# RMS norm of 16384 rows on one core: the whole of x kept in SBUF, the gain multiplied first, the row scale written back over x, and every mean square but the first two rows' on ScalarE

## The chip, the cores and the metric

One core of one Trainium2 chip runs the program. The metric is the device time of one execution in microseconds (us); several runs are given by their median. Names of engines in the rows: PE is TensorE, DVE is VectorE, ACT is ScalarE, POOL is GpSimd, SP is SyncE, which only issues transfers here.

## What is computed

The reference, cut to what matters. x is 512x32x640 and g is 640, both bfloat16:

```python
rms = jnp.sqrt((x * x).mean(axis=-1, keepdims=True) + 1e-6)
return x / rms * g
```

So each of the 16384 rows of 640 numbers is divided by the root of its mean square, and multiplied by g column by column. x is 20.97 MB, read once, and the output is as large, written once.

## The kernel before

The 16384 rows are laid out 128 to a step: partition p holds rows 128p to 128p+127 of x, and what is called a **row** below is one such step, 128 partitions x 640 bfloat16 (1280 bytes a partition, 163.84 KB in all). There are 128 of them. `chunk_schedule` cuts them into 19 chunks of 2, 4, 4, fourteen times 8, 4 and 2 rows. For each chunk the loop at L154 does this:

- **Load** (L92, L159, issued by SP): a chunk goes into one of 6 buffers `x_sb_full`. From the seventh load on SP waits until the buffer's earlier chunk has been read by DVE and PE.
- **Mean squares**, one row at a time, into a column of `ms`. Most rows go by PE and ACT: two matmuls with an identity matrix (L200 and L203, 512 and 128 columns) copy the row into one of 3 PSUM tiles `xp`, and ACT squares that with an accumulated sum (L209), its elementwise result going to a throw-away SBUF tile `junk_a`. 24 of the 128 rows (`n_dve`, L162 to L172) go to DVE instead, as one `scalar_tensor_tensor` (L187).
- **1/rms**: ACT takes the root (L231, into `rstd`), DVE the reciprocal (L233).
- **Scale**: DVE multiplies each row by its 1/rms (L143, one `tensor_scalar` a row, into `o_sb_full`, 3 buffers) and then the whole chunk by g in place (L145, one `tensor_tensor` a chunk).
- **Store**: one transfer a chunk, issued by POOL (L149), by SP for the last three chunks (L147).

g is loaded as one row and spread over the partitions by a matmul with ones (L119) and two copies on ACT (L122). The order on each engine is not written out: the tile framework's scheduler chooses it, and so a `scalar_tensor_tensor` of one chunk may stand between the steps of another. ACT, DVE and PE run their instructions strictly in that order.

Of the kernel before, what the change touches and what calls it, by code (L numbers as in the profile page):

```python
# [6 lines left out]

# [3 lines left out]
J_MAX = int(os.environ.get("K_J", "8"))
RAMP = [int(v) for v in os.environ.get("K_RAMP", "2,4").split(",") if v]
DRAMP = [int(v) for v in os.environ.get("K_DRAMP", "4,2").split(",") if v]
DVE_SS_EVERY = float(os.environ.get("K_DVE_EVERY", "6"))
FRONT = [int(v) for v in os.environ.get("K_FRONT", "2,2,2").split(",") if v]
NODVE_LAST = int(os.environ.get("K_NODVE_LAST", "3"))
IO_BUFS = int(os.environ.get("K_BUFS", "6"))
O_BUFS = int(os.environ.get("K_OBUFS", "3"))
S_BUFS = int(os.environ.get("K_SBUFS", "4"))  # L20
OUT_ENG = os.environ.get("K_OUTENG", "gpsimd")
IN_ENG = os.environ.get("K_INENG", "sync")
G_ENG = os.environ.get("K_GENG", "sync")
LASTOUT_SYNC = int(os.environ.get("K_LASTOUT_SYNC", "3"))
GBC = os.environ.get("K_GBC", "pe_act")
X0FIRST = int(os.environ.get("K_X0FIRST", "2"))
PAIR = int(os.environ.get("K_PAIR", "0"))
WARM_SQRT = int(os.environ.get("K_WARM", "1"))
XPSUM = int(os.environ.get("K_XPSUM", "3"))


def chunk_schedule(R):
    start = list(RAMP)
    end = list(DRAMP)
    if sum(start) + sum(end) > R:
        start, end = [], []
    rem = R - sum(start) - sum(end)
    mid = []
    while rem >= J_MAX:
        mid.append(J_MAX)  # L40
        rem -= J_MAX
    if rem:
        mid = [rem] + mid
    sizes = start + mid + end
    assert sum(sizes) == R
    return sizes
# [3 lines left out]
def kernel(  # L50
# [16 lines left out]
    assert N % P == 0, f"{N=} must be a multiple of {P}"  # L67
# [5 lines left out]
    sizes = chunk_schedule(R)
    JM = max(sizes)
    nchunks = len(sizes)
# [4 lines left out]
    junk_pool = ctx.enter_context(tc.tile_pool(name="junk", bufs=int(os.environ.get("K_JBUFS", "8"))))  # L80
    small = ctx.enter_context(tc.tile_pool(name="small", bufs=S_BUFS))

    engines = {"sync": nc.sync, "scalar": nc.scalar, "gpsimd": nc.gpsimd, "vector": nc.vector}
    in_eng = engines[IN_ENG]
    out_eng = engines[OUT_ENG]

    pre_x = {}
    r0p = 0
    for ci0 in range(min(X0FIRST, nchunks)):
        J0 = sizes[ci0]  # L90
        x_sb_full0 = xin_pool.tile([P, JM, D], xf.dtype, name="x_sb_full")
        in_eng.dma_start(out=x_sb_full0[:, :J0, :], in_=x_v[:, r0p:r0p + J0, :])  # L92
        pre_x[ci0] = x_sb_full0
        r0p += J0

    eps_sb = consts.tile([P, 1], f32)
    nc.vector.memset(eps_sb[:], EPS)  # L97

    if WARM_SQRT:
        warm = consts.tile([P, 1], f32)  # L100
        nc.vector.memset(warm[:], 1.0)
        warm2 = consts.tile([P, 1], f32)
        nc.scalar.activation(out=warm2[:], in_=warm[:], func=ACT.Sqrt, bias=eps_sb[:], scale=1.0)  # L103

    g_sb = consts.tile([P, D], g.dtype)
    if GBC == "dma":
        g_src = bass.AP(tensor=g.tensor, offset=g.offset, ap=[[0, P], g.ap[-1]])
        engines[G_ENG].dma_start(out=g_sb[:], in_=g_src)
    else:
        g1 = consts.tile([1, D], g.dtype)  # L110
        g_row = bass.AP(tensor=g.tensor, offset=g.offset, ap=[[0, 1], g.ap[-1]])
        engines[G_ENG].dma_start(out=g1[:], in_=g_row)  # L112
        ones1 = consts.tile([1, P], bf16)
        nc.vector.memset(ones1[:], 1.0)
        gps_pool = ctx.enter_context(tc.tile_pool(name="gps", bufs=1, space=bass.MemoryType.PSUM))
        half = D // 2
        for h in range(2):
            gp = gps_pool.tile([P, half], f32, name=f"gp{h}")
            nc.tensor.matmul(out=gp[:], lhsT=ones1[:], rhs=g1[:, h * half:(h + 1) * half],  # L119
                             start=True, stop=True)  # L120
            if GBC == "pe_act":
                nc.scalar.copy(out=g_sb[:, h * half:(h + 1) * half], in_=gp[:])  # L122
            else:
                nc.vector.tensor_copy(out=g_sb[:, h * half:(h + 1) * half], in_=gp[:])

    if XPSUM:
        from concourse.masks import make_identity
        ident = consts.tile([P, P], bf16, name="ident")
        make_identity(nc, ident)
        xps_pool = ctx.enter_context(tc.tile_pool(name="xps", bufs=XPSUM, space=bass.MemoryType.PSUM))  # L130

# [137 lines left out]
```

## Time and profile before

| what | value |
|---|---|
| time, median of 6 runs | 119.71 us (119.22 to 120.71) |
| the profiled execution: time | 119.74 us |
| the profiled execution: span from first to last instruction | 118.0 us |
| DVE busy | 102.9 us, 87% of the span, 217 instructions |
| ACT busy | 78.6 us, 67%, 231 instructions |
| PE busy | 59.8 us, 51% |
| POOL busy | 11.2 us, 9% |
| DMA | 42.00 MB, 356 GB/s over the span |
| read and written in HBM | 20.97 MB each |
| mean granted TensorE clock | 0.703 of full speed |

A view of the profile either sums over the span (busy time of each engine, groups of instructions by line), or cuts it into stretches, or lists instructions in order of time with the idle time before each and what ended it. The busy time of an instruction includes its start-up and its end, in which the next one already runs: what an engine needs for a series is the distance from start to start, not the sum of the busy times.

### The profile page before, as it was taken

What the parts mean: (1) busy time and instruction counts of PE and PEld (TensorE: products, weight loads), DVE (VectorE), ACT (ScalarE), POOL (GpSimd) and SP (SyncE); (2) the same over time, 40 slices, a digit from 0 to 9 for tenths busy, and PEclk for the clock granted to TensorE, in tenths of its full rate; (3) what the DMA queues carried; (4) which work ended last, traced back from release to release, by engine and by line L of the source; (5) the groups of instructions that cost most, each with busy time, mean ns of one, the idle gap of its engine ahead of it and who ended that gap; (6) DMA issues with size and microseconds to landing.
All of it is one profiled execution on the core that took longest, in us unless ns stands there. A gap on an engine that the chain in (4) does not pass through costs nothing.

```text
span 118.0 us, 1065 instructions
## 1 busy us (share of the span) xinstructions
PE 59.8 (51%) x210; PEld 23.2 (20%) x210; DVE 102.9 (87%) x217; ACT 78.6 (67%) x231; POOL 11.2 (9%) x22
## 2 busy tenths in 40 slices
PE   0244889655895593969492859484993000000000
PEld 0011333222332221323131323132331000000000
DVE  0598998999999999998949957959699999999870
ACT  5076699999999995979695979697999120000000
POOL 2002021010101010100101010010020102033000
PEclk9999999999769955555559555569559655555555
DMA  3999999999999999999999999999719190825994
GB/s 90 344 347 410 394 425 424 422 430 432 431 417 434 434 422 413 441 437 406 434 441 433 406 441 434 417 422 443 249 56 396 58 389 0 358 87 222 431 373 196
DMA packets 5415, 42.00 MB, mean 356 GB/s; under 512 B 609, under 2 KB 610, under 8 KB 1826
## 3 DMA queue, kind: packets, MB, share of 16 engines
q1 hardware_dynamic: 3170, 23.27, 48.5%
q0 software_dynamic: 2240, 18.68, 37.7%
...
HBM read 20.97 MB, written 20.97 MB: 356 GB/s over the span
## 4 chain that ended last, share of the span: by engine, by line
issue 52%; DVE 14%; DMA 12%; ACT 12%; POOL 4%; SPq 1%; PE 1%; POOLq 0%
ACT junk_a L209 11%; DMA x_sb_full<-in_x_dram 8%; DVE o_sb_full L145 7%; DVE o_sb_full L143 5%; POOL out_dram L149 4%; DMA out_dram<-o_sb_full 4%; DVE junk_d L187 1%; SPq L92 1%; PE xp L200 1%; ACT rstd L231 0%; DVE rstd L233 0%; SPq L159 0%; SPq L112 0%; POOLq L149 0%; PE xp L203 0%
## 5 line engine op out<-in xcount | busy, mean ns | idle before, releaser
L209 ACT ACTIVATE junk_a<-xp 128x640 bf16<-128x640 f32 x104 | 72.1, 764 | 9.9 <-PE xp L203 9.8
L200 PE MATMUL xp<-x_sb_full,ident 128*128 128x512 bf16 x104 | 52.7, 528 | 24.8 <-DMA x_sb_full<-in_x_dram 16.2
L145 DVE TENSOR_TENSOR o_sb_full<-o_sb_full,g_sb 128x5120 bf16<-128x5120 bf16 (+2 forms) x19 | 45.4, 2391 | 0.0
L143 DVE TENSOR_SCALAR o_sb_full<-x_sb_full,rstd 128x640 bf16<-128x640 bf16 x128 | 39.8, 380 | 0.4 <-DVE o_sb_full L143 0.4
L203 PE MATMUL xp<-x_sb_full,ident 128*128 128x128 bf16 x104 | 29.3, 282 | 0.0
L209 ACT ACTIVATION_READ_ACCUMULATOR junk_a<-xp 128x1 f32 x104 | 28.0, 269 | 0.0
L187 DVE SCALAR_TENSOR_TENSOR junk_d<-x_sb_full 128x640 bf16<-128x640 bf16 x24 | 19.1, 801 | 3.2 <-DMA x_sb_full<-in_x_dram 3.1
L200 PEld LDWEIGHTS <-ident 128*128 128x128 bf16 x104 | 13.4, 129 | 41.1 <-DMA x_sb_full<-in_x_dram 19.5
L149 POOL DMA_DIRECT2D out_dram<-o_sb_full x16 | 10.5, 655 | 95.3 <-DVE o_sb_full L145 66.8
L203 PEld LDWEIGHTS <-ident 128*128 128x128 bf16 x104 | 11.4, 110 | 20.1 <-issue 19.8
L231 ACT ACTIVATE rstd<-ms,eps_sb 128x8 f32<-128x8 f32 (+2 forms) x19 | 5.9, 327 | 8.3 <-DVE junk_d L187 8.3
L233 DVE RECIPROCAL rstd<-rstd 128x8 f32<-128x8 f32 (+2 forms) x19 | 3.4, 187 | 7.1 <-ACT rstd L231 7.1
L119 PE MATMUL gp_88<-g_81,ones_83 1*128 1x320 bf16 x1 | 0.4, 419 | 5.2 <-DMA g_81<-in_g_dram 5.2
L187 DVE DVE_READ_ACCUMULATOR junk_d<-x_sb_full 128x1 f32 x24 | 2.0, 81 | 0.0
L103 ACT ACT_TABLE_LOAD x1 | 1.3, 1283 | 0.7 <-PEq L253 0.7
L119 PEld LDWEIGHTS <-ones_83 1*128 1x128 bf16 x2 | 0.2, 99 | 5.1 <-issue 4.0
L97 DVE MEMSET eps_sb<- 128x1 f32 x1 | 0.1, 59 | 0.8 <-PEq L253 0.8
L119 PE MATMUL gp_91<-g_81,ones_83 1*128 1x320 bf16 x1 | 0.5, 466 | 0.0
L122 ACT CAST g_sb<-gp_91 128x320 bf16<-128x320 f32 x1 | 0.4, 427 | 0.0
L122 ACT CAST g_sb<-gp_88 128x320 bf16<-128x320 f32 x1 | 0.4, 405 | 0.0
L103 ACT ACTIVATE warm_78<-warm,eps_sb 128x1 f32<-128x1 f32 x1 | 0.3, 295 | 0.0
masks.py:199 POOL TENSOR_SCALAR_AFFINE_SELECT ident<-ident 128x128 bf16<-128x128 bf16 x1 | 0.3, 287 | 0.1
(7 smaller groups left out, 0.8 us busy)
## 6 DMA issues: line engine op xcount, KB each, us to landing
...
```

What stands on the lines that cost most here:

```text
L92: in_eng.dma_start(out=x_sb_full0[:, :J0, :], in_=x_v[:, r0p:r0p + J0, :])
L103: nc.scalar.activation(out=warm2[:], in_=warm[:], func=ACT.Sqrt, bias=eps_sb[:], scale=1.0)
L119: nc.tensor.matmul(out=gp[:], lhsT=ones1[:], rhs=g1[:, h * half:(h + 1) * half], start=True, stop=True)
L143: nc.vector.tensor_scalar_mul(out=o_sb[:, j, :], in0=x_sb[:, j, :], scalar1=rstd[:, roff + j:roff + j + 1])
L145: nc.vector.tensor_tensor(out=o_sb, in0=o_sb, in1=g_bcast(J), op=ALU.mult)
L149: out_eng.dma_start(out=o_v[:, r0:r0 + J, :], in_=o_sb)
L187: nc.vector.scalar_tensor_tensor(out=junk_d[:], in0=x_sb[:, j, :], scalar=inv_d, in1=x_sb[:, j, :], op0=ALU.mult, op1=ALU.mult, accum_out= ...
L200: nc.tensor.matmul(out=xp[:, :c1], lhsT=ident[:], rhs=x_sb[:, j, :c1], start=True, stop=True)
L203: nc.tensor.matmul(out=xp[:, c1:], lhsT=ident[:], rhs=x_sb[:, j, c1:], start=True, stop=True)
L209: nc.scalar.activation(out=junk_a[:], in_=sq_in, func=ACT.Square, scale=inv_sqrt_d, accum_out=ms[:, moff + j:moff + j + 1],)
L231: nc.scalar.activation(out=rstd[:, :J], in_=ms[:, :J], func=ACT.Sqrt, bias=eps_sb[:], scale=1.0)
L233: nc.vector.reciprocal(out=rstd[:, :J], in_=rstd[:, :J])
```

## The change

The kernel is rewritten. What each part does:

- **Loads**: 13 tiles `x0` to `x12`, one for each load, hold all 128 rows for the whole run. The loads are of 2, 4, 4, 8, six times 16, 8, 4 and 2 rows; a load of 16 rows is two chunks, so the chunks are the same 19 as before. No load waits for a buffer.
- **Mean squares**: the two rows of chunk 0 stay on DVE (L102). The other 126 go through PE and ACT. ACT's square writes its elementwise result over `xp` in PSUM, in float32, in place of an SBUF tile, and its sum into a PSUM tile `ms`. The root (L123) reads `ms` from PSUM.
- **Scale**: DVE multiplies a chunk by g first, from x into a buffer `y` (L129, 3 buffers), which needs no mean square; then it multiplies each row of `y` by 1/rms (L136) into the place that the row of x had.
- **Store**: from the x tiles, all 19 by POOL (L137).
- **Order**: written by hand for PE, DVE, SP and POOL. DVE does `times_g` of chunk c, and then `finish` of chunk c-1.

```diff
+LOADS = [
+    [2], [4], [4], [8], [8, 8],
+    [8, 8], [8, 8], [8, 8], [8, 8],
+    [8, 8], [8], [4], [2],
+]
...
-    xin_pool = ctx.enter_context(tc.tile_pool(name="xin", bufs=IO_BUFS))
-    out_pool = ctx.enter_context(tc.tile_pool(name="xout", bufs=O_BUFS))
...
+    xin = ctx.enter_context(tc.tile_pool(name="xin", bufs=1))
+    ypool = ctx.enter_context(tc.tile_pool(name="ypool", bufs=3))
...
+    xps = ctx.enter_context(tc.tile_pool(name="xps", bufs=3, space=bass.MemoryType.PSUM))
+    mps = ctx.enter_context(tc.tile_pool(name="mps", bufs=2, space=bass.MemoryType.PSUM))
...
+    ctx.enter_context(tc.manual_schedule(
+        engines={ENG.PE, ENG.DVE, ENG.SP, ENG.Pool}))
...
+    for i, cuts in enumerate(LOADS):
+        n = sum(cuts)
+        t = xin.tile([P, n, D], xf.dtype, name=f"x{i}")
+        nc.sync.dma_start(out=t[:], in_=x_v[:, r0:r0 + n, :])
+        if i == 0:
+            nc.sync.dma_start(out=g1[:], in_=g_row)
...
+    def sumsq(c):
+        xs, J, _ = chunks[c]
+        if c == 0:
...
+        ms = mps.tile([P, JM], f32, name="ms")
...
         for j in range(J):
+            xp = xps.tile([P, D], f32, name="xp")
+            for lo, hi in ((0, 512), (512, D)):
+                nc.tensor.matmul(out=xp[:, lo:hi], lhsT=ident[:], rhs=xs[:, j, lo:hi],
+                                 start=True, stop=True)
+            sq = nc.scalar.activation(out=xp[:], in_=xp[:], func=ACT.Square, scale=inv_sqrt_d,
+                                      accum_out=ms[:, j:j + 1])
...
+    def times_g(c):
+        xs, J, _ = chunks[c]
+        y = ypool.tile([P, JM, D], bf16, name="y")
+        nc.vector.tensor_tensor(out=y[:, :J, :], in0=xs, in1=g_bcast(J), op=ALU.mult)
+        return y
 
+    def finish(c, y, r):
+        xs, J, r0 = chunks[c]
+        nc.vector.reciprocal(out=r[:, :J], in_=r[:, :J])
+        for j in range(J):
+            nc.vector.tensor_scalar_mul(out=xs[:, j, :], in0=y[:, j, :], scalar1=r[:, j:j + 1])
+        nc.gpsimd.dma_start(out=o_v[:, r0:r0 + J, :], in_=xs)
...
+    prev = None
+    for c in range(len(chunks)):
+        ms = sumsq(c)
+        y = times_g(c)
+        r = rms(c, ms)
+        if prev is not None:
+            finish(*prev)
+        prev = (c, y, r)
+    finish(*prev)
```

Three places of the order of instructions follow. First DVE in the middle of the program, before, over two chunks of 8 rows:

```order
L233 RECIPROCAL rstd<-rstd 128x8
L187 SCALAR_TENSOR_TENSOR junk_d,ms<-x_sb_full 128x640
L143 TENSOR_SCALAR o_sb_full<-x_sb_full,rstd 128x640 x8
L187 SCALAR_TENSOR_TENSOR junk_d,ms<-x_sb_full 128x640
L145 TENSOR_TENSOR o_sb_full<-o_sb_full,g_sb 128x5120
L233 RECIPROCAL rstd<-rstd 128x8
```

And DVE in the changed program at the same place (the numbers tell the tiles apart: `x4_93` is the tile of the fifth load, `x5_95` that of the sixth):

```order
L129 TENSOR_TENSOR y_306<-x4_93,g_sb_117 128x5120
L134 RECIPROCAL rstd_261<-rstd_261 128x8
L136 TENSOR_SCALAR x4_93<-y_259,rstd_261 128x640 x8
L129 TENSOR_TENSOR y_353<-x5_95,g_sb_117 128x5120
L134 RECIPROCAL rstd_308<-rstd_308 128x8
L136 TENSOR_SCALAR x4_93<-y_306,rstd_308 128x640 x8
```

The two `scalar_tensor_tensor` between the steps of a chunk are gone, and the product with g has moved ahead of the root: `y_353`, a chunk of the next load, stands before the reciprocal and the eight row scales of the chunk ahead of it.

Second, SP's loads from the fifth on, before, with the semaphores that each waits for (DMAHW and DMASW are those of transfers that SP and POOL issued):

```order
L159 DMA x_sb_full<-in_x_dram 128x5120 x3
L159 DMA x_sb_full<-in_x_dram 128x5120 [waits DMAHW0_49,DVE_49]
L159 DMA x_sb_full<-in_x_dram 128x5120 [waits DMAHW1_49,DVE_49,PE_49]
L159 DMA x_sb_full<-in_x_dram 128x5120 [waits DMAHW3_49,DVE_49,PE_49]
L159 DMA x_sb_full<-in_x_dram 128x5120 [waits DMAHW2_49,DMAHW4_49,DVE_49,PE_49]
```

and in the changed program:

```order
L70 DMA x_91<-in_x_dram 128x5120
L70 DMA x_93<-in_x_dram 128x10240
L70 DMA x_95<-in_x_dram 128x10240
L70 DMA x_97<-in_x_dram 128x10240
L70 DMA x_99<-in_x_dram 128x10240 [waits DMAHW0_49]
L70 DMA x_101<-in_x_dram 128x10240 [waits DMAHW1_49]
```

The waits for DVE and PE are gone. What is left (the semaphore of the load eight transfers earlier) is that of the first loads, which are the first to land.

Third, ACT in the changed program around the end of one chunk and the beginning of the next (`ms_183` is the chunk of 8 rows of the fourth load, `ms_226` the first of the fifth):

```order
L113 ACTIVATE xp_208,ms_183<-xp_208 128x640
L113 ACTIVATE xp_212,ms_183<-xp_212 128x640
L113 ACTIVATE xp_227,ms_226<-xp_227 128x640
L123 ACTIVATE rstd_218<-ms_183,eps_sb_113 128x8
L113 ACTIVATE xp_231,ms_226<-xp_231 128x640
```

The root of a chunk stands behind the first square of the next chunk, as it did in many chunks before; that square needs the next chunk's load.

## Rows read from the trace of the kernel before

**Rows 1.** The page: busy tenths in 40 slices of 2.95 us.
```profile
DVE  0598998999999999998949957959699999999870
DMA  3999999999999999999999999999719190825994
```
**Rows 2.** Stretches: us, busy (instructions) of PE, PEld, DVE, ACT, POOL; clock, DMA, GB/s.
```profile
0.00:12.00 12.00, 3.09 (x10) 1.09 (x10) 7.45 (x24) 5.88 (x15) 1.38 (x7) 1.00 0.83 301
12.00:82.00 70.00, 49.56 (x178) 19.54 (x179) 64.52 (x136) 62.10 (x183) 6.01 (x11) 0.73 1.01 426
82.00:118.00 36.00, 7.12 (x22) 2.57 (x21) 30.89 (x60) 10.58 (x34) 3.79 (x4) 0.55 0.59 239
...
107.50:114.00 6.50, 0.00 (x0) 0.00 (x0) 6.10 (x9) 0.00 (x0) 0.00 (x0) 0.50 0.97 403
...
116.50:117.00 0.50, 0.00 (x0) 0.00 (x0) 0.00 (x0) 0.00 (x0) 0.00 (x0) 0.50 0.08 26
```
**Rows 3.** Waits: engine, line, what it waited for: us in total, times, longest.
```profile
SPq L159 <- DVE o_sb_full L143: 74.1, 13, 8.3
```
**Rows 4.** Groups by line: busy us, mean ns of one, idle before.
```profile
L187 DVE SCALAR_TENSOR_TENSOR junk_d<-x_sb_full 128x640 bf16<-128x640 bf16 x24 | 19.1, 801 | 3.2 <-DMA x_sb_full<-in_x_dram 3.1
```
**Rows 5.** DVE in order of time: start, us, instruction.
```profile
10.88 0.18 DVE L233 RECIPROCAL rstd<-rstd 128x4 f32<-128x4 f32 x1 [0.18 <-ACT rstd L231]
11.09 1.27 DVE L143 TENSOR_SCALAR o_sb_full<-x_sb_full,rstd 128x640 bf16<-128x640 bf16 x4
...
93.37 2.46 DVE L143 TENSOR_SCALAR o_sb_full<-x_sb_full,rstd 128x640 bf16<-128x640 bf16 x8
95.74 0.82 DVE L187 SCALAR_TENSOR_TENSOR junk_d<-x_sb_full 128x640 bf16<-128x640 bf16 x1
96.48 2.82 DVE L145 TENSOR_TENSOR o_sb_full<-o_sb_full,g_sb 128x5120 bf16<-128x5120 bf16 x1
99.22 0.20 DVE L233 RECIPROCAL rstd<-rstd 128x8 f32<-128x8 f32 x1
...
113.12 0.38 DVE L143 TENSOR_SCALAR o_sb_full<-x_sb_full,rstd 128x640 bf16<-128x640 bf16 x1
113.54 0.82 DVE L145 TENSOR_TENSOR o_sb_full<-o_sb_full,g_sb 128x1280 bf16<-128x1280 bf16 x1
```
**Rows 6.** ACT in order of time.
```profile
13.00 0.70 ACT L209 ACTIVATE junk_a<-xp 128x640 bf16<-128x640 f32 x1 [1.14 <-PE xp L203]
...
13.60 0.19 ACT L209 ACTIVATION_READ_ACCUMULATOR junk_a<-xp 128x1 f32 x1
...
...
22.15 0.74 ACT L209 ACTIVATE junk_a<-xp 128x640 bf16<-128x640 f32 x1
22.82 0.35 ACT L231 ACTIVATE rstd<-ms,eps_sb 128x8 f32<-128x8 f32 x1
23.02 0.75 ACT L209 ACTIVATE junk_a<-xp 128x640 bf16<-128x640 f32 x1
```
**Rows 7.** PE in order of time: the first matmul on the fourth load.
```profile
12.25 0.61 PE L200 MATMUL xp<-x_sb_full,ident 128*128 128x512 bf16 x1 [1.88 <-DMA x_sb_full<-in_x_dram]
```
**Rows 8.** DMA queues from 13 to 30 us: packets, MB, share of 16 engines.
```profile
q1 hardware_dynamic: 582, 5.29, 74.0%
q0 software_dynamic: 391, 1.87, 26.5%
```
**Rows 9.** DMA queues from 40 to 60 us, the same columns.
```profile
q1 hardware_dynamic: 478, 4.39, 51.8%
q0 software_dynamic: 468, 4.19, 49.5%
```
**Rows 10.** The issue of stores on POOL: ns min/median/max; then the last one, and DVE beside it.
```profile
L149 POOL DMA_DIRECT2D out_dram<-o_sb_full x16: 531/531/1896, 9.3 to 105.2; - x16
...
105.23 1.90 POOL L149 DMA_DIRECT2D out_dram<-o_sb_full  x1 [4.98 <-DVE o_sb_full L145]
...
104.86 2.15 DVE L143 TENSOR_SCALAR o_sb_full<-x_sb_full,rstd 128x640 bf16<-128x640 bf16 x7
```
**Rows 11.** The chain that ended last: that store from its issue to its landing.
```profile
105.23 4.93 DMA out_dram<-o_sb_full
```

More of the change, by code (lines that the diff above doesn't have):

```diff
@@ L7 @@
 from concourse._compat import with_exitstack
-import os
+from concourse.masks import make_identity
 EPS = 1e-6
[L12 to L46, printed above, removed]
+LOADS = [
[3 more added lines that the diff above has]
+]
 @with_exitstack
@@ L66 @@
     N, D = xf.shape
[L67 removed]
+    assert N % P == 0
     R = N // P
+    assert sum(sum(l) for l in LOADS) == R
+    JM = max(max(l) for l in LOADS)
     x_v = xf.rearrange("(p r) d -> p r d", p=P)
     o_v = of.rearrange("(p r) d -> p r d", p=P)
[L73 to L75 removed]
     consts = ctx.enter_context(tc.tile_pool(name="consts", bufs=1))
[L78 removed]
@@ L79 @@
-    out_pool = ctx.enter_context(tc.tile_pool(name="xout", bufs=O_BUFS))
[L80 to L130, printed above, removed]
+    xin = ctx.enter_context(tc.tile_pool(name="xin", bufs=1))
+    ypool = ctx.enter_context(tc.tile_pool(name="ypool", bufs=3))
+    junk = ctx.enter_context(tc.tile_pool(name="junk", bufs=2))
+    small = ctx.enter_context(tc.tile_pool(name="small", bufs=4))
@@ new lines @@
+    chunks = []
+    r0 = 0
+    for i, cuts in enumerate(LOADS):
[4 more added lines that the diff above has]
+            nc.sync.dma_start(out=g1[:], in_=g_row)
+        off = 0
+        for J in cuts:
+            chunks.append((t[:, off:off + J, :], J, r0 + off))
+            off += J
+        r0 += n
+    ones1 = consts.tile([1, P], bf16, name="ones1")
+    nc.vector.memset(ones1[:], 1.0)
@@ new lines @@
+    eps_sb = consts.tile([P, 1], f32, name="eps_sb")
+    nc.vector.memset(eps_sb[:], EPS)
+    warm = consts.tile([P, 1], f32, name="warm")
+    nc.scalar.activation(out=warm[:], in_=eps_sb[:], func=ACT.Sqrt, bias=eps_sb[:], scale=1.0)
+    g_sb = consts.tile([P, D], g.dtype, name="g_sb")
+    gp = xps.tile([P, D], f32, name="xp")
+    for lo, hi in ((0, 512), (512, D)):
+        nc.tensor.matmul(out=gp[:, lo:hi], lhsT=ones1[:], rhs=g1[:, lo:hi], start=True, stop=True)
+    nc.scalar.copy(out=g_sb[:], in_=gp[:])
@@ new lines, in rms @@
+    def rms(c, ms):
+        J = chunks[c][1]
+        r = small.tile([P, JM], f32, name="rstd")
+        nc.scalar.activation(out=r[:, :J], in_=ms[:, :J], func=ACT.Sqrt, bias=eps_sb[:], scale=1.0)
+        return r
+    def times_g(c):
[6 more added lines that the diff above has]
+        nc.vector.reciprocal(out=r[:, :J], in_=r[:, :J])
+        for j in range(J):
+            nc.vector.tensor_scalar_mul(out=xs[:, j, :], in0=y[:, j, :], scalar1=r[:, j:j + 1])
+        nc.gpsimd.dma_start(out=o_v[:, r0:r0 + J, :], in_=xs)
```

109 lines of the change are left out of this document (17 added, 92 removed).

## The prediction

> **What bounds the kernel now.** I read the busy tenths over the span first, then the stretches, then the waits, then the two busy engines in order of time. The tenths show two regimes. Up to slice 28 (82 us) the DMA row stands at 9; behind that it is broken, while DVE goes on at 9 until just before the end [rows 1]. The stretches give the sizes: from 12 to 82 us the DMA engines are full at 426 GB/s, and from 82 to 118 us they move only 239 GB/s, with DVE busy 30.89 of 36 us [rows 2]. So first the DMA engines are the limit, and then, with the loads done, the stores come at DVE's pace. SP waited 74.1 us in 13 waits for DVE to free a load's buffer [rows 3]; but since the DMA engines were full all that time, an earlier issue could not have brought the bytes earlier. The buffers cost nothing by themselves. What costs is that DVE still has those 30.89 us of work when the loads end.
>
> Why it is behind: beside scale and product it does 24 `scalar_tensor_tensor`, 19.1 us [rows 4]. Read from start to start, a chunk of 8 rows takes DVE 2.37 us for eight row scales (93.37 to 95.74), 0.74 for each `scalar_tensor_tensor` (95.74 to 96.48) and 2.74 for the product with g (96.48 to 99.22) [rows 5].
>
> The profiled execution took 119.74 us for a span of 118.0, so 1.74 lie outside it; the median of the runs is 119.71, and I make the sum against the profiled one without a correction.
>
> **The change part by part.**
>
> *Mean squares off DVE.* 22 of the 24 `scalar_tensor_tensor` go: 22 x 0.74 = 16.3 us of DVE's time. A chunk of 8 then costs DVE the product 2.74, the reciprocal with the wait of the first row scale for it 0.21 (10.88 to 11.09) and the row scales 2.37: 5.32 us [rows 5]. For 14 such chunks and five small ones that is some 86 us in place of 103.
>
> *The same 22 on ACT and PE.* A square with the read of its sum takes ACT 0.67 us from start to start (22.15 to 22.82), a root 0.20 (22.82 to 23.02) [rows 6]. 126 squares and 19 roots are 84.6 + 3.7 = 88 us, and 8 rows take 5.57 us. So ACT, not DVE, sets the pace of the computation, by 0.25 us a chunk.
>
> *The square's result into PSUM, over its input.* No instruction of before writes to PSUM from ACT. From below: the step cannot be worth more than the time that the read of the sum leaves, which the sum by bytes (below) makes worth nothing. From above: if a square could no longer overlap the one ahead of it, its 0.70 and the 0.19 of the read would add up to 0.89 [rows 6]. I take 0.67, since the number of elements is the same, and the row it is nearest to is the square itself, which already reads PSUM. On ACT's destination the Trainium skill (ScalarE: Activation LUTs, section "ACT is a hardware spline evaluator") says that writing to PSUM is faster than writing to SBUF. No row here shows it; by it the square would be at or under 0.67, and the sum would not move.
>
> *Product with g first.* The same instruction on the same shape; the work moves, and 2.74 us of it leave the way from a root to its store. Row scales now each wait for PE and each signal; before, eight shared one signal. From below this costs nothing, since PE read those rows a chunk earlier. From above, a row scale followed by a step that waits for it takes 0.42 us (113.12 to 113.54) in place of 0.30 [rows 5]: 0.12 x 128 = 15 us. I take nothing, as these waits are for work long done.
>
> *What is queued behind a late load.* The product of chunk c stands ahead of the scales of chunk c-1, and the root of c-1 behind the first square of c. A load that is late so holds back the chunk ahead of it as well. That happens at the start: the fourth load was readable at 12.25, its first square ran at 13.0 [rows 6, 7], and it keeps ACT busy until 18.6. The fifth, now of 16 rows, ends with row 34: 5.57 MB. By 12 us 301 x 12 = 3.61 MB had moved [rows 2], so its bytes are through at 16.6 us if it had the engines alone, and at 20.4 if all 10 rows of earlier stores (1.64 MB) went ahead; landing and the matmuls take about 2 us more. ACT waits between 0 and 4 us; I take 2. Later no load is late if loads get ahead of stores. Between 13 and 30 us, with both queued, loads moved 5.29 MB and stores 1.87 [rows 8], the loads in pieces of 10 KB, the stores first in pieces of 5; between 40 and 60, both in pieces of 10 KB, 4.39 and 4.19 [rows 9]. I read that as turns by piece. Now loads come in rows of 20 KB and stores of 10, so loads should get about two thirds. The 94 rows behind the fifth load are 15.4 MB, 36 us alone and 54 at two thirds of 426 GB/s: the loads are through between 56 and 74 us.
>
> *Stores.* They stay on POOL, three more than before. Each is issued in 0.531 us, but the one issued while DVE ran row scales took 1.896 [rows 10]. Behind 17 of the 19 stores DVE now turns to a product, and a late issue there meets a queue of stores anyway; the last two can lose up to 1.4 us each. I take 0 and keep 2.8 as the upper end. A rule of the Trainium skill speaks against this part: SBUF — State Buffer, section "SBUF: two separate sides", says that POOL cannot write its transfers' descriptors while DVE runs certain fast forms, of which the row scale would be one. The slow issue agrees with it; by the rule alone the sum would grow by those 2.8 us.
>
> **The sum.** Two floors, and the later one is the end.
>
> By bytes: 41.94 MB in all, 3.61 of them by 12 us, the other 38.33 at 426 GB/s: 90.0 us, so the last byte at 102.0. Stores alone, though, ran at 403 GB/s (107.5 to 114 us) [rows 2]; if the last 30 us are stores alone, 1.7 us more: 103.7. From the last byte (about 116.6) to the end of the span before passed 1.4 us [rows 2]. Span 103.4 to 105.1.
>
> By ACT: 18.6 + 2 + 110 squares of 0.67 + 15 roots of 0.20 = 97.3; the last root, reciprocal and two row scales 1.1; a store of 8 rows on POOL took 4.93 us to land [rows 11], of which 1.31 MB at 426 GB/s are 3.1, so 2 rows take 1.8 + 0.8; with the closing, the span ends at about 102.5.
>
> The bytes are the later by 1 to 2 us. Since the last stores stand in that queue, I take a span of 104.5, and with 1.74 a time of **106.2 us**, 11% less than before.
>
> **The rivals.**
>
> *ACT gets slower* through the in-place write in PSUM. Its slack is 1 to 2 us, some 15 ns a square; beyond that each 10 ns costs 1.26 us. At 0.72 us a square it is 104.2 + 6.3 = 110.5 (104.2 is ACT's floor of 102.5 with the 1.74), at the upper bound of 0.89 it is 104.2 + 126 x 0.22 = 132. The end on the other side: from 0.80 us a square the kernel is slower than before (104.2 + 126 x 0.123 = 119.7). For it speaks that nothing of before shows the write; against it that the elements and the input stay. 12% for 108 to 118, 7% for no gain or a loss.
>
> *DVE becomes the bound* through the wait and signal of each row scale: up to 6.3 us a chunk against ACT's 5.57, 0.75 x 14 = 10: up to 116. 8% for 109 to 116.
>
> *Loads get no lead*: turns are even, 16 rows take 2 x 2.62 MB / 0.43 = 12.2 us, while ACT needs 11.1; over the six large loads it starves for up to 6.6 us less its slack of 2: 108 to 111. The even split of 40 to 60 us speaks for it, the one of 13 to 30 against. 8%. POOL's slow last issues would end within it (109).
>
> *The loads' rate falls*, so that the bytes alone undo the gain. The Trainium skill (DMA: Bandwidth & Descriptors, section "Where 436 GB/s comes from") says that the memory side limits transfers between HBM and SBUF to about 358 GB/s for a core. As a mechanism here: 41.94 MB at that rate, 117 us, from 2 us on, and 3.1 of closing: 122. The 426 GB/s over 70 us deny it [rows 2]. 1%.
>
> *The change as named does nothing*: were the wait for buffers the whole of it, the result would be 119.7, since the DMA engines were full anyway. DVE's lost 16 us speak against that. 2%.
>
> **How the numbers follow.** The forecast (104 to 108) has 62%. The range must reach into the rivals above it: 104.0 to 112.5 adds the even turns (8%) and about half of the cases of a slower ACT and DVE (10%), 80% together; below 104.0 bytes would have to move faster than 426 GB/s. About 1% is what a measurement of this kernel can tell from no change. Faster by over 1%: 62 + 8 + 12 + 8, less 2 for what I have not seen: 88%. Within 1%: 4%. Slower: 8%.
>
> **What would show it.** The DMA row full until about 100 us and loads through before 74; squares 0.67 us apart; row scales 0.30 us apart; DVE and ACT done near 98 us, with stores left in the queue; one wait of PE for the fifth load near 19 us. It is wrong if squares stand 0.70 us apart or more, if DVE has no idle time, or if PE waits for loads after 30 us.

## The result and the profile after

The changed kernel takes **106.61 us** (median of 10 runs, 105.92 to 106.98) where the kernel before takes 119.74 beside it: a ratio of 0.889 (0.886 to 0.891). The profiled execution took 106.19 us for a span of 104.4, so 1.79 us lie outside it. Medians here and below are of all runs of a kernel; ratios leave out three runs in a slower state of the chip, two of e8_changed_again and one of e10_six_buffers_again.

The page, in 40 slices of 2.6 us, to be laid beside [rows 1]:

```profile
DVE  0598990899999979999999999999999999999100
ACT  6269997699999999999999999999999999992000
DMA  2999899999999999999999999999999999999980
```

The broken end of the DMA row is gone: it stands at 9 until the last slices, and DVE and ACT are both through before it. The stretches of [rows 2], with the same columns:

```profile
0.00:12.00 12.00, 5.37 (x22) 2.29 (x23) 7.87 (x18) 8.07 (x22) 1.41 (x8) 1.00 0.87 331
12.00:82.00 70.00, 44.23 (x202) 19.31 (x201) 65.34 (x119) 68.24 (x216) 6.89 (x13) 0.98 1.01 426
82.00:105.00 23.00, 6.92 (x32) 2.96 (x31) 14.49 (x37) 12.69 (x41) 2.67 (x5) 0.77 0.86 359
```

From 12 to 82 us nothing changed for the DMA engines: 426 GB/s, as before. Nearly all of the gain lies behind 82 us (in the first 12 us 331 GB/s in place of 301 moved 0.36 MB more, worth 0.85 us). DVE had 30.89 us of work left there, now it has 14.49. DVE in order of time (start, us, instruction, idle before), to be laid beside [rows 5]:

```profile
14.59 1.27 DVE L136 TENSOR_SCALAR x_89<-y,rstd 128x640 bf16<-128x640 bf16 x4
18.69 2.83 DVE L129 TENSOR_TENSOR y<-x_93,g_sb 128x5120 bf16<-128x5120 bf16 x1 [2.83 <-DMA x_93<-in_x_dram]
21.43 0.20 DVE L134 RECIPROCAL rstd<-rstd 128x8 f32<-128x8 f32 x1
21.74 2.46 DVE L136 TENSOR_SCALAR x_91<-y,rstd 128x640 bf16<-128x640 bf16 x8
24.11 2.82 DVE L129 TENSOR_TENSOR y<-x_93,g_sb 128x5120 bf16<-128x5120 bf16 x1
...
96.16 0.81 DVE L136 TENSOR_SCALAR x_109<-y,rstd 128x640 bf16<-128x640 bf16 x2
```

A chunk of 8 rows takes 24.11 - 18.69 = 5.42 us: the product 2.74, from the reciprocal to the first row scale 0.31, the row scales 2.37. Behind the first load, DVE's only wait of more than 0.6 us is the one for the fifth. ACT at the same place (beside [rows 6]), and then its roots near the end:

```profile
19.26 0.69 ACT L113 ACTIVATE xp<-xp 128x640 f32<-128x640 f32 x1 [1.76 <-PE xp L111]
19.91 0.27 ACT L123 ACTIVATE rstd<-ms,eps_sb 128x8 f32<-128x8 f32 x1
20.06 0.72 ACT L113 ACTIVATE xp<-xp 128x640 f32<-128x640 f32 x1
...
21.36 0.73 ACT L113 ACTIVATE xp<-xp 128x640 f32<-128x640 f32 x1
21.99 0.76 ACT L113 ACTIVATE xp<-xp 128x640 f32<-128x640 f32 x1
...
24.53 0.86 ACT L113 ACTIVATE xp<-xp 128x640 f32<-128x640 f32 x1
25.16 0.46 ACT L123 ACTIVATE rstd<-ms,eps_sb 128x8 f32<-128x8 f32 x1
25.31 0.90 ACT L113 ACTIVATE xp<-xp 128x640 f32<-128x640 f32 x1
...
84.74 0.79 ACT L123 ACTIVATE rstd<-ms,eps_sb 128x8 f32<-128x8 f32 x1
...
90.18 0.79 ACT L123 ACTIVATE rstd<-ms,eps_sb 128x8 f32<-128x8 f32 x1
```

The busy time of a square grows from 0.69 to 0.90 in these lines and to 1.34 later, because it runs while the next one has begun. While it grows, the starts run ahead of the work: 3.17 us for the five squares from 21.36 to 24.53, 0.634 each, a root 0.15, and 25.31 - 20.06 = 5.25 us for a chunk. From end to end a chunk takes 5.45 us: the root that starts at 19.91 ends at 20.18, the next at 25.62, and the two near the end at 85.53 and 90.97. So a square takes 0.66. From 36 us on the busy time has stopped growing, and the starts say the same (90.18 - 84.74 = 5.44). ACT so needs 0.04 us more for a chunk than DVE, whose next chunks take 5.41. A distance from start to start, as used ahead of the prediction, tells what an engine needs only where the busy time does not grow.

The queues from 13 to 30 us and, in the second fence, from 40 to 60 us (packets, MB, share), beside [rows 8, 9]; q1 carries the loads that SP issued, q0 the stores that POOL issued:

```profile
q1 hardware_dynamic: 319, 5.88, 80.9%
q0 software_dynamic: 312, 1.43, 20.3%
```

```profile
q1 hardware_dynamic: 320, 5.63, 65.6%
q0 software_dynamic: 327, 2.91, 34.6%
```

The packets go one to one, and the bytes by the size of a piece (what one transfer moves for one partition: 20 KB for a load of 16 rows, 10 KB for a store of 8).

### The profile page after: what moved, and what is told of

It is laid out like the page before. It is cut to its first block, busy times and chain, and to the rows that moved or that the text cites. A ratio compares the mean times of both kernels' runs of the same rounds, so it can differ in the third digit from the quotient of the medians.

```text
span 104.4 us, 1183 instructions
## 1 busy us (share of the span) xinstructions
PE 56.5 (54%) x254; PEld 24.6 (24%) x254; DVE 87.7 (84%) x172; ACT 89.0 (85%) x274; POOL 11.0 (11%) x25
## 4 chain that ended last, share of the span: by engine, by line
issue 53%; DMA 15%; ACT 13%; POOL 6%; DVE 2%; SPq 2%; POOLq 1%; PE 1%; ACTq 0%
DMA x_93<-in_x_dram 15%; ACT xp L113 12%; POOL out_dram L137 6%; DVE x_95 L136 2%; SPq L70 2%; PE xp L111 1%; ACT rstd L123 1%; POOLq L173 1%; POOLq L137 0%; SPq L72 0%; ACTq L123 0%; ACTq L113 0%
## 5 line engine op out<-in xcount | busy, mean ns | idle before, releaser
L113 ACT ACTIVATE xp<-xp 128x640 f32<-128x640 f32 x126 | 85.7, 1131 | 2.5 <-PE xp L111 2.5
L113 ACT ACTIVATION_READ_ACCUMULATOR xp<-xp 128x1 f32 x126 | 69.5, 603 | 0.0
L123 ACT ACTIVATE rstd<-ms,eps_sb 128x8 f32<-128x8 f32 (+2 forms) x18 | 11.6, 642 | 0.0
L111 PE MATMUL xp<-x_93,ident 128*128 128x512 bf16 (+1 forms) x32 | 7.8, 346 | 4.9 <-DMA x_93<-in_x_dram 2.7
L111 PE MATMUL xp<-x_103,ident 128*128 128x512 bf16 (+1 forms) x32 | 6.9, 297 | 4.0 <-ACT xp L113 4.0
L111 PE MATMUL xp<-x_99,ident 128*128 128x512 bf16 (+1 forms) x32 | 6.9, 297 | 4.0 <-ACT xp L113 4.0
L111 PE MATMUL xp<-x_101,ident 128*128 128x512 bf16 (+1 forms) x32 | 6.9, 297 | 4.0 <-ACT xp L113 4.0
L111 PE MATMUL xp<-x_95,ident 128*128 128x512 bf16 (+1 forms) x32 | 6.9, 297 | 4.0 <-ACT xp L113 4.0
L111 PE MATMUL xp<-x_97,ident 128*128 128x512 bf16 (+1 forms) x32 | 6.9, 297 | 4.0 <-ACT xp L113 4.0
L129 DVE TENSOR_TENSOR y<-x_93,g_sb 128x5120 bf16<-128x5120 bf16 x2 | 5.6, 2822 | 2.8 <-DMA x_93<-in_x_dram 2.8
L129 DVE TENSOR_TENSOR y<-x_101,g_sb 128x5120 bf16<-128x5120 bf16 x2 | 5.6, 2822 | 0.0
L129 DVE TENSOR_TENSOR y<-x_99,g_sb 128x5120 bf16<-128x5120 bf16 x2 | 5.6, 2821 | 0.0
L129 DVE TENSOR_TENSOR y<-x_95,g_sb 128x5120 bf16<-128x5120 bf16 x2 | 5.6, 2820 | 0.0
L129 DVE TENSOR_TENSOR y<-x_97,g_sb 128x5120 bf16<-128x5120 bf16 x2 | 5.6, 2818 | 0.0
L129 DVE TENSOR_TENSOR y<-x_103,g_sb 128x5120 bf16<-128x5120 bf16 x2 | 5.6, 2818 | 0.0
L136 DVE TENSOR_SCALAR x_95<-y,rstd 128x640 bf16<-128x640 bf16 x16 | 4.9, 380 | 0.7 <-PE xp L111 0.5
L136 DVE TENSOR_SCALAR x_99<-y,rstd 128x640 bf16<-128x640 bf16 x16 | 4.9, 383 | 0.2
L136 DVE TENSOR_SCALAR x_97<-y,rstd 128x640 bf16<-128x640 bf16 x16 | 4.9, 382 | 0.2
L136 DVE TENSOR_SCALAR x_103<-y,rstd 128x640 bf16<-128x640 bf16 x16 | 4.9, 382 | 0.2
L136 DVE TENSOR_SCALAR x_93<-y,rstd 128x640 bf16<-128x640 bf16 x16 | 4.9, 381 | 0.2
L136 DVE TENSOR_SCALAR x_101<-y,rstd 128x640 bf16<-128x640 bf16 x16 | 4.9, 380 | 0.2
```

The costliest lines, as they stand in the source:

```text
L111: nc.tensor.matmul(out=xp[:, lo:hi], lhsT=ident[:], rhs=xs[:, j, lo:hi], start=True, stop=True)
L113: sq = nc.scalar.activation(out=xp[:], in_=xp[:], func=ACT.Square, scale=inv_sqrt_d, accum_out=ms[:, j:j + 1])
L123: nc.scalar.activation(out=r[:, :J], in_=ms[:, :J], func=ACT.Sqrt, bias=eps_sb[:], scale=1.0)
L129: nc.vector.tensor_tensor(out=y[:, :J, :], in0=xs, in1=g_bcast(J), op=ALU.mult)
L136: nc.vector.tensor_scalar_mul(out=xs[:, j, :], in0=y[:, j, :], scalar1=r[:, j:j + 1])
```

## The experiments

The theory was that DVE's 22 extra `scalar_tensor_tensor` had cost the time, and that behind them the bytes set the end. Rival 1: the gain comes from loads that wait for no buffer. Rival 2: the computation is still the end. Rival 3: the write into PSUM and the order are what matters. The kernel before took 119.7 to 120.0 us beside these runs; ratios are to it. In the table, "before" and "changed" name the kernel that was altered.

| run | what differs | us | ratio (95%) |
|---|---|---|---|
| changed kernel | | 106.61 | 0.889 (0.886 to 0.891) |
| e8_changed_again | nothing | 106.88 | 0.889 (0.884 to 0.894) |
| e1_squares_off_dve | before, 22 rows' mean squares to ACT | 111.86 | 0.934 (0.931 to 0.937) |
| e2_loads_wait_for_no_buffer | before, x resident | 119.95 | 1.000 (0.998 to 1.003) |
| e4_squares_back_on_dve | changed, those 22 back on DVE | 117.82 | 0.985 (0.979 to 0.991) |
| e3_square_into_sbuf | changed, ACT's square into SBUF | 108.03 | 0.900 (0.894 to 0.906) |
| e9_scale_before_product | changed, product behind the scale | 109.54 | 0.912 (0.905 to 0.918) |
| e7_loads_of_8_rows | changed, no load over 8 rows | 107.14 | 0.893 (0.888 to 0.898) |
| e10_six_buffers_again | changed, x in 6 buffers | 107.25 | 0.894 (0.888 to 0.899) |
| e5_four_stores_fewer | changed, 5.24 MB not written | 105.62 | 0.881 (0.875 to 0.886) |
| e6_loads_and_stores_alone | changed, no computation | 105.82 | 0.881 (0.877 to 0.885) |
| e12_last_stores_by_sp | changed, last 3 stores by SP | 106.04 | 0.886 (0.881 to 0.891) |
| e11_first_loads_and_last_stores | the same, and other first loads | 105.92 | 0.884 (0.880 to 0.888) |

### The mean squares alone, in the kernel before

```diff
-DVE_SS_EVERY = float(os.environ.get("K_DVE_EVERY", "6"))
-FRONT = [int(v) for v in os.environ.get("K_FRONT", "2,2,2").split(",") if v]
+DVE_SS_EVERY = float(os.environ.get("K_DVE_EVERY", "0"))
+FRONT = [int(v) for v in os.environ.get("K_FRONT", "2").split(",") if v]
```

> The kernel before with one part of the change alone: the mean squares of all rows but the first two go by PE and ACT (2 scalar_tensor_tensor on DVE in place of 24). Loads keep their 6 buffers, the product with g stays behind the row scale, ACT's square writes to SBUF. Theory 1 (DVE's 22 scalar_tensor_tensor were the cost, 16.3 us, and behind them the bytes set the end at 106): 106 to 110 us, 107.5 the likeliest, since the loads' waits for buffers are hidden by full DMA engines. Rival 1 (the gain came from loads that wait for no buffer): 117 to 120 us. Rival 3 (the square's write into PSUM and the order by hand are needed for the gain): over 112 us, with ACT's squares 0.67 us apart and ACT the last to end.

111.86: 8.0 us less, so the larger part of the gain comes from this alone, and rival 1 falls. But it is 5.3 us over the changed kernel, above the range of theory 1 and just under rival 3's 112. Its waits show why the buffers of the loads are not the reason, and DVE's waits and rows where the rest is:

```profile
SPq L159 <- DVE o_sb_full L143: 67.4, 13, 6.4
DVE o_sb_full L143 <- DVE rstd L233: 4.3, 7, 0.7
DVE o_sb_full L143 <- issue: 1.0, 1, 1.0
```

```profile
18.94 0.20 DVE L233 RECIPROCAL rstd<-rstd 128x8 f32<-128x8 f32 x1 [2.65 <-ACT rstd L231]
19.18 2.46 DVE L143 TENSOR_SCALAR o_sb_full<-x_sb_full,rstd 128x640 bf16<-128x640 bf16 x8
21.68 2.83 DVE L145 TENSOR_TENSOR o_sb_full<-o_sb_full,g_sb 128x5120 bf16<-128x5120 bf16 x1
24.61 0.20 DVE L233 RECIPROCAL rstd<-rstd 128x8 f32<-128x8 f32 x1
...
49.02 2.46 DVE L143 TENSOR_SCALAR o_sb_full<-x_sb_full,rstd 128x640 bf16<-128x640 bf16 x8 [0.67 <-DVE rstd L233]
...
104.63 0.83 DVE L145 TENSOR_TENSOR o_sb_full<-o_sb_full,g_sb 128x1280 bf16<-128x1280 bf16 x1
```

SP still waits 67.4 us for buffers, and yet ACT, squares 0.68 us apart and never out of work behind 7 us, waited 0.1 us in all before its squares. At 18.94 DVE stands idle for a root, and has the whole chunk, product too, still ahead of it; then, until 36 us, a chunk takes 5.67 us, at ACT's pace.

From 36 to 85 us DVE falls behind that pace, with 6.1 us for most chunks. The first row scale of a chunk waits 0.3 to 1.0 us, 5.3 us in eight waits. The view names the reciprocal, which was done; but seven of these row scales begin 0.08 us behind the landing of the store of three chunks earlier (49.02, where the store issued at 36.13 lands at 48.94; 79.49, where one lands at 79.41). There are 3 output buffers, so a chunk has to wait until such a store has left its buffer, and the full DMA engines need 6.14 us for one chunk in and one out (2.62 MB at 427 GB/s). DVE is through at 105.5, the changed kernel's DVE at 96.97. So here the computation is again the later end: from 92 us on the DMA engines move only 238 GB/s. How much of the distance to the changed kernel is due to the output buffers this run does not tell by itself; e10_six_buffers_again below has as many of them, with the product first.

### Resident x alone, in the kernel before

```diff
-    xin_pool = ctx.enter_context(tc.tile_pool(name="xin", bufs=IO_BUFS))
+    xin_pool = ctx.enter_context(tc.tile_pool(name="xin", bufs=1))
...
-            x_sb_full = xin_pool.tile([P, JM, D], xf.dtype, name="x_sb_full")
+            x_sb_full = xin_pool.tile([P, J, D], xf.dtype, name=f"x_sb_{ci}")
```

> The kernel before with the other part alone: every chunk of x has a tile of its own, so that no load waits for a buffer; the 24 scalar_tensor_tensor stay on DVE (the throw-away tiles are 2 in place of 8, to make room). Theory 1: 117 to 120 us, SP's 74 us of waiting gone without a gain, the loads through earlier and DVE's remaining work the longer behind them. Rival 1: 105 to 110 us.

119.95, a ratio of 1.000. The wait of [rows 3] is gone: at L159 SP now waits for earlier loads alone (first line). The stretch behind 82 us reads as before, with 30.13 us of DVE.

```profile
SPq L159 <- DMA x_sb<-in_x_dram: 37.1, 10, 6.1
```

```profile
82.00:118.00 36.00, 7.52 (x24) 2.74 (x22) 30.13 (x57) 10.42 (x33) 3.62 (x4) 0.55 0.57 236
```

### The mean squares back on DVE, in the changed kernel

```diff
-        ms = mps.tile([P, JM], f32, name="ms")
+        ms = small.tile([P, JM], f32, name="ms")
...
+            if j >= J - n_dve:
+                jd = junk.tile([P, D], bf16, name="junk_d")
+                sq = nc.vector.scalar_tensor_tensor(
+                    out=jd[:], in0=xs[:, j, :], scalar=inv_d, in1=xs[:, j, :],
+                    op0=ALU.mult, op1=ALU.mult, accum_out=ms[:, j:j + 1])
...
```

The sums of a chunk stand in SBUF here, since both engines write them.

> The changed kernel with the other part undone: the 24 rows that went by scalar_tensor_tensor before go there again (22 more on DVE; the column of sums stands in SBUF). Loads still wait for no buffer, the product with g still stands first. Theory 1: DVE needs 16.3 us more, 5.41 + 0.74 x 1.33 = 6.4 us a chunk, ends near 97 + 16 = 113 and the time is 113 + 2.6 for the last store + 3.1 of closing = 117 to 120 us. Rival 1 (buffers): at most 109 us.

117.82. With nearly everything else of the change in place only 2.0 us of the 13.1 are left; taking the squares off DVE is worth 11.2 us here, and 8.0 in the kernel before. DVE's last instruction stands 12.4 us later than in the changed kernel (108.59 against 96.16): the term of 16.3 us, less waiting that it fills, of which 2.8 stood ahead of the fifth load.

```profile
108.59 0.68 DVE L154 TENSOR_SCALAR x<-y,rstd 128x640 bf16<-128x640 bf16 x2
```

### The square's destination

```diff
-            sq = nc.scalar.activation(out=xp[:], in_=xp[:], func=ACT.Square, scale=inv_sqrt_d,
+            ja = junk.tile([P, D], bf16, name="junk_d")
+            sq = nc.scalar.activation(out=ja[:], in_=xp[:], func=ACT.Square, scale=inv_sqrt_d,
```

> The changed kernel with one part undone: ACT's square writes its elementwise result to a bf16 tile in SBUF (2 buffers) in place of over its input in PSUM. If the destination alone made the squares 0.635 us apart, they stand 0.67 apart here, ACT needs 126 x 0.038 = 4.8 us more and sets the pace of the computation in DVE's place by 0.14 us a chunk. Theory 1 (the bytes are the end): 106.2 to 107.5 us, the last square up to 4 us later. Rival 2 (the computation is the end): 109 to 111 us. If the distance stays 0.635, the destination was not what shortened it.

108.03, some 1.4 us more, between the ranges of theory 1 and of rival 2. ACT near the end:

```profile
84.26 1.15 ACT L114 ACTIVATE junk_d<-xp 128x640 bf16<-128x640 f32 x1
84.94 1.15 ACT L114 ACTIVATE junk_d<-xp 128x640 bf16<-128x640 f32 x1
...
86.95 0.71 ACT L124 ACTIVATE rstd<-ms,eps_sb 128x8 f32<-128x8 f32 x1
87.10 1.16 ACT L114 ACTIVATE junk_d<-xp 128x640 bf16<-128x640 f32 x1
```

The squares stand 0.68 us apart, from start to start and from end to end, where the changed kernel's stand 0.66 apart from end to end. A chunk takes ACT 5.59 us between the ends of two roots, all along, in place of 5.45: the destination alone makes that difference. The root stays at 0.15, since the sums still stand in PSUM; with the sums in SBUF (e4_squares_back_on_dve) it took 0.20. ACT is then clearly the later one, and DVE waits for it near the end:

```profile
93.28 0.20 DVE L135 RECIPROCAL rstd<-rstd 128x8 f32<-128x8 f32 x1 [1.42 <-ACT rstd L124]
```

ACT's last square begins 2.3 us later than in the changed kernel (95.47 against 93.15): 0.14 for each of 13 chunks, and a start 0.44 us later behind the fifth load. That is half of what was expected, since the expectation took 0.038 us a square, from starts; by the ends it is 0.02. DVE's chunk took 5.41 us at 51.74 and 5.59, ACT's pace, at 73.62, and DVE ends 2.3 us later too.

### The order of scale and product

```diff
-        nc.vector.tensor_tensor(out=y[:, :J, :], in0=xs, in1=g_bcast(J), op=ALU.mult)
...
-            nc.vector.tensor_scalar_mul(out=xs[:, j, :], in0=y[:, j, :], scalar1=r[:, j:j + 1])
+            nc.vector.tensor_scalar_mul(out=y[:, j, :], in0=xs[:, j, :], scalar1=r[:, j:j + 1])
+        nc.vector.tensor_tensor(out=xs, in0=y[:, :J, :], in1=g_bcast(J), op=ALU.mult)
```

> The changed kernel with the order on DVE undone: each chunk is scaled by 1/rms first and multiplied by g behind that, both after the root, as in the kernel before. DVE has 2.74 us less to do while it waits for the first roots and so ends some 3 to 4 us later, near 100.5. Theory 1: the last store then stands 1 to 2 us behind the bytes: 106.5 to 108.5 us; of the 5.3 us between the kernel before without its scalar_tensor_tensor (111.9) and the changed one, the product's place is about half. If the order is of no weight: 106.2 to 106.9 us; if it is all of it: 110 us and more.

109.54, 2.9 us more: a little over the range. The place is the one seen in e1_squares_off_dve:

```profile
12.18 0.18 DVE L133 RECIPROCAL rstd<-rstd 128x4 f32<-128x4 f32 x1 [4.61 <-ACT rstd L123]
...
21.27 0.20 DVE L133 RECIPROCAL rstd<-rstd 128x8 f32<-128x8 f32 x1 [3.01 <-ACT rstd L123]
...
26.81 0.20 DVE L133 RECIPROCAL rstd<-rstd 128x8 f32<-128x8 f32 x1
27.04 2.46 DVE L135 TENSOR_SCALAR y<-x,rstd 128x640 bf16<-128x640 bf16 x8
29.61 2.83 DVE L136 TENSOR_TENSOR x<-y,g_sb 128x5120 bf16<-128x5120 bf16 x1
```

DVE waits 4.6 and 3.0 us for early roots, with nothing else to do. (In this profile the second load also landed 2 us later than in the changed kernel's, 7.8 against 5.7, which has a part in the 4.6.) A chunk takes 26.81 - 21.27 = 5.54 us, and not 5.42, since the product waits for the last row scale (2.57 us to it in place of 2.37). DVE ends at 103.6, 6.6 us later; 2.9 of them reach the median time, and 4.0 that of this profiled execution. The product first is therefore no mere re-ordering: it is work that DVE can do before any root is there.

### Loads without a lead, and buffers again

```diff
-    [2], [4], [4], [8], [8, 8],
-    [8, 8], [8, 8], [8, 8], [8, 8],
-    [8, 8], [8], [4], [2],
+    [2], [4], [4], [8], [8], [8], [8], [8], [8], [8],
+    [8], [8], [8], [8], [8], [8], [8], [4], [2],
```

> The changed kernel with its six loads of 16 rows cut into twelve of 8, so that loads and stores both move in rows of 10 KB. If the two queues take turns by piece, packets and now bytes too go 1 to 1 while both are queued, and the loads are through near 85 to 90 us in place of 76. Theory 1 (the DMA engines never stand still, and the order in which the bytes go is of no weight): 106.2 to 108 us. The prediction's rival (without a lead the loads starve ACT): 108 to 111 us, with waits of PE for loads behind 30 us of 2 us and more in total. The fifth load, half as large, should land near 16 in place of 18.7 us, so that ACT waits less there.

The queues from 40 to 60 us (packets, MB, share), then DVE late in the program:

```profile
q0 software_dynamic: 466, 4.27, 50.5%
q1 hardware_dynamic: 464, 4.24, 50.2%
```

```profile
72.96 2.83 DVE L128 TENSOR_TENSOR y<-x,g_sb 128x5120 bf16<-128x5120 bf16 x1 [0.61 <-DMA x<-in_x_dram]
...
79.08 2.83 DVE L128 TENSOR_TENSOR y<-x,g_sb 128x5120 bf16<-128x5120 bf16 x1 [0.62 <-DMA x<-in_x_dram]
```

Turns by piece are shown: with equal pieces, equal bytes. The loads did starve the computation, at 79.08 - 72.96 = 6.12 us a chunk, which is 2 x 1.31 MB at 429 GB/s (60 to 82 us). But it cost 0.5 us, inside the intervals of both. Two things in the trace speak for why. The starving came late and was short: DVE waited 1.8 us in three products, the first at 72.96. And the fifth load, half as long, landed at 16.2 in place of 18.7, so that DVE's wait of 2.8 us for it is gone. That the engines carry loads while no store is there to move is argued, and not shown apart from these.

The second kernel puts these loads into 6 buffers, and the row scales into 3 output tiles:

```diff
-    xin = ctx.enter_context(tc.tile_pool(name="xin", bufs=1))
+    xin = ctx.enter_context(tc.tile_pool(name="xin", bufs=6))
+    opool = ctx.enter_context(tc.tile_pool(name="opool", bufs=3))
...
```

> The changed kernel without the residence of x: loads of 8 rows go into 6 buffers, as before, and wait for DVE and PE to have read them; row scales write to 3 output tiles; the product with g first, ACT's square in PSUM and the order by hand stay. Its nearest neighbour is the changed kernel with loads of 8 rows (107.1 us). Theory 1 (loads that wait for no buffer are worth nothing, as in the kernel before): 106.6 to 108 us. Rival 1 (they are worth something once DVE is relieved): over 109 us, with waits of PE for loads behind 30 us.

107.25, as with resident x. SP waits again for the readers of its buffers, PE and DVE, and DVE for stores to leave its output tiles (us, times, longest), at no price that can be measured.

```profile
SPq L72 <- PE xp L112: 29.9, 12, 3.1
SPq L72 <- DVE y L130: 26.6, 13, 3.6
DVE o L138 <- DMA out_dram<-o: 5.3, 6, 1.3
```

DVE waits as long for output as in e1_squares_off_dve, and the time is 4.6 us less. So those waits do not make e1's 5.3 us by themselves; the product's place (2.9 us) and the square's destination (1.4), undone one by one, come to 4.3 of them.

### Fewer bytes, and no computation

```diff
-        nc.gpsimd.dma_start(out=o_v[:, r0:r0 + J, :], in_=xs)
+        if c not in (6, 9, 12, 15):
+            nc.gpsimd.dma_start(out=o_v[:, r0:r0 + J, :], in_=xs)
```

> The changed kernel without the stores of four chunks of 8 rows in the middle (chunks 6, 9, 12 and 15): 5.24 MB less to write, that part of the output is not written; loads and all work on PE, ACT and DVE stay. Theory 1 (the bytes are the end): 5.24 MB at 426 GB/s are 12.3 us less for the DMA engines, so that the computation becomes the end: DVE through at 97 us as in the changed kernel, the last store of two rows 2.6 us to land, 1.4 of closing and 1.74 outside the span: 102 to 103.5 us. Rival 2 (the computation already is the end): 106.2 to 107 us, unchanged.

105.62: not the 3 to 4 us less of theory 1, and not nothing. DVE ends at 97.2, as in the changed kernel. The last stretches (columns as in [rows 2]):

```profile
94.00:95.00 1.00, 0.00 (x0) 0.00 (x0) 0.89 (x4) 0.97 (x4) 0.53 (x1) 1.00 0.00 0
95.00:96.00 1.00, 0.00 (x0) 0.00 (x0) 1.00 (x4) 0.02 (x1) 0.00 (x0) 1.00 0.78 328
...
100.00:101.00 1.00, 0.00 (x0) 0.00 (x0) 0.00 (x0) 0.00 (x0) 0.00 (x0) 0.50 1.04 399
101.00:102.00 1.00, 0.00 (x0) 0.00 (x0) 0.00 (x0) 0.00 (x0) 0.00 (x0) 0.50 0.16 62
```

The DMA engines stand idle from 89 to 95, and then need until past 101 for what the computation releases at its end: the last three stores, 14 rows and 2.29 MB, issued between 94.4 and 98.1. So the computation, with nothing ahead of its last stores in the queue, ends at 105.6. Both ranges were missed.

The opposite run leaves the computation out: the loop only stores each chunk once it has landed.

```diff
-        ms = sumsq(c)
-        y = times_g(c)
...
+        xs, J, r0 = chunks[c]
+        nc.gpsimd.dma_start(out=o_v[:, r0:r0 + J, :], in_=xs)
```

> The changed kernel's loads and stores with the same sizes and queues and no computation: mean squares, roots, products and row scales are left out, each chunk is stored as it was loaded once its load has landed. Theory 1: the same 42 MB are 98.5 us at 426 GB/s, from 2 us on, with 3.1 us of closing: 103.5 to 106 us, at most 3 us below the changed kernel. Rival 2 (the computation is the end): under 103 us.

105.82. So the bytes alone end at 105.8, and rival 2, in the form that the computation alone is the end, falls. The two ends differ by less than the spread of either run, and the changed kernel stands 0.8 to 1.0 us above both.

### Two tries to go below

```diff
+        eng = nc.sync if c >= len(chunks) - 3 else nc.gpsimd
+        eng.dma_start(out=o_v[:, r0:r0 + J, :], in_=xs)
```

> The changed kernel with its last three stores (8, 4 and 2 rows) issued by SP, as before, and not by POOL. Between the last byte and the end of the span lie 2.2 us in the changed kernel and 1.4 in the kernel before, whose last store SP issued. If who issues sets that difference: 0.5 to 0.8 us less, 105.8 to 106.2. If the last of POOL's own stores, now the one of the chunk ahead, ends as late in the shared queue: 106.4 to 106.9.

The second has that too, and other first loads:

```diff
+    [2], [4], [4], [8], [8], [8], [8],
+    [8, 8], [8, 8], [8, 8], [8, 8],
+    [8, 8], [4], [2],
...
+        (nc.scalar if i == 1 else nc.sync).dma_start(out=t[:], in_=x_v[:, r0:r0 + n, :])
```

> A version meant to be faster than the changed kernel. The last three stores by SP; three loads of 8 rows ahead of the loads of 16 (so that no load is 16 rows long before DVE has work to wait with); the second load and g issued by ACT beside SP's first. Theory 1: the bytes, 105.8 us by the run of loads and stores alone, begin 0.3 us earlier and close 0.7 us earlier; the computation, 105.6 by the run with four stores fewer, loses up to 2.8 us of DVE's wait for the fifth load: 104.6 to 105.6 us. If the start and the end of the transfers do not move: 106.2 to 106.9.

106.04 and 105.92: 0.3 and 0.5% under the changed kernel by their ratios, whose intervals overlap. The second is perhaps half a per cent faster, and not shown to be; it lies between its two ranges. In it DVE no longer waits for the fifth load and issues its last row scales at 95.44 in place of 96.16, but the first load landed later (5.26 in place of 3.86 us), with the second beside it on another queue. Both come to where the bytes alone end, 105.8. That run had its last stores from POOL, so what is left to gain with the last stores from SP is not shown.

## Why the prediction held, step by step

The time came out at 106.6 for 106.2, and the mechanism as put: DVE relieved, then DMA engines full to the end. That it came within 0.4 us is in part luck: several sizes were off and cancelled, and the path of the computation was another than I had it.

- **The buffers cost nothing by themselves**: right, in the kernel before (e2_loads_wait_for_no_buffer, 1.000) and in the changed one (e10_six_buffers_again).
- **16.3 us off DVE**: right as a term (e4_squares_back_on_dve). Its worth depends on the rest: 8.0 us in the kernel before, 11.2 in the changed one.
- **The square at 0.67 us, 5.57 a chunk**: near, but by a reading that does not hold for ACT. From end to end a chunk takes 5.67 us with the kernel before's writes (e1_squares_off_dve), 5.59 with the square to SBUF and the sums in PSUM (e3_square_into_sbuf), and 5.45 in the changed kernel; there the square is 0.66 and the root 0.15 in place of 0.20. The Trainium skill (ScalarE: Activation LUTs, section "ACT is a hardware spline evaluator") says that ACT writes faster to PSUM; the pair of runs agrees, 0.66 against 0.68 us for a square. I held that the sum would not move by it. Undoing it costs 1.4 us, so it does. (126 x 0.67 is 84.4 and 19 x 0.20 is 3.8; the 88 stands.)
- **ACT sets the pace by 0.25 us a chunk**: the sign is right, the size is not, and the path was DVE's. ACT takes 5.45 and DVE 5.41, which I sized 5.32: the first row scale stands 0.31 us behind its reciprocal, not 0.21. DVE waited 2.83 us for the fifth load, and its reciprocal stood 1.25 us behind the end of ACT's root from then on (21.43 and 20.18). ACT, losing 0.04 us a chunk, did not use that up before the last chunk of 8 rows (reciprocal at 91.01, root ended at 90.97). So my own sign of being wrong came: but for 0.55 us at 38.41, DVE has no idle time behind the fifth load. In e10_six_buffers_again, where DVE does not wait for that load, it goes at ACT's 5.45 from 18 to 50 us.
- **Product first moves 2.74 us off the way from root to store**: right, but I gave it no price. It costs 2.9 us to undo, through DVE's early waits and 0.12 us more a chunk.
- **Row scales with a wait each cost nothing**: right for the eight, 2.37 us as before, so that rival fell. But the first stands 0.31 us behind the reciprocal where the row scales write over x, and 0.23 and 0.24 where they write elsewhere and need not wait for PE (e9_scale_before_product, e10_six_buffers_again): some 0.07 us a chunk, 1 us in all. The one long wait for PE, at 38.41, was 0.55.
- **The fifth load, 2 us late for ACT**: ACT waited 1.76, DVE 2.83. PE waits for no load behind 30 us.
- **Turns by piece, loads at two thirds**: right, 65.6% of the engines from 40 to 60 us, though [rows 8], with 582 packets to 391, had not shown it. The loads were through at 76.2 (the last, issued at 18.68, took 57.5 us to land), and not before 74: I had all 94 rows in pieces of 20 KB, and the last 14, in pieces of 10, 5 and 2.5 KB, took from 61.7 to 76.2.
- **POOL's issue**: all 19 took at most 0.68 us, none the 1.896 of [rows 10]. Nearly all fall beside a product; the one at 96.28 falls beside row scales and took 0.53 as well. In e9_scale_before_product, where they fall beside row scales, the median is 0.653 in place of 0.531. The Trainium skill's rule (SBUF — State Buffer, section "SBUF: two separate sides") would have it wait for DVE's instruction; here that is 0.12 us at most times. No run shows 1.9 more than once among its stores, and in e6_loads_and_stores_alone, with DVE idle, five took 1.05, so what made the one of 1.896 stays open.
- **Floor by bytes, span 103.4 to 105.1**: right (104.4; e6_loads_and_stores_alone 103.7). Two of its terms cancelled. By 12 us 331 x 12 = 3.97 MB had moved, not 3.61, worth 0.85 us. From the last byte (about 102.3) to the end passed 2.1 us, not the 1.4 of [rows 2].
- **Floor by computation, span 102.5**: mis-sized; e5_four_stores_fewer has 103.8. The computation itself was through sooner than I had it (DVE 97.2, my sum 98.4). The way behind it was 6.6 us, where I counted 4.0: I let the last two rows' store land by itself, while it stands behind the eight and four rows ahead of it, issued only 3.2 and 1.0 us before (94.36, 96.56, 97.54); and the closing again. So "the bytes are the later by 1 to 2 us" failed: the two are level.
- **Rivals**: a slower ACT, a DVE held by its waits, and a lower rate fell. Even turns were made in e7_loads_of_8_rows, and the price, 2 to 5 us, was too high. My step let the loads starve ACT over all six large loads and added that to the end; but the three long waits came only behind 72 us, 1.8 us together, and the shorter fifth load gave 2.8 back.

What stays open: the 0.8 us that the changed kernel takes above either floor. No run tells whether it is the two meeting at the end or the order of the transfers.
